# A quarter of the taps moved ahead of the filter's load in a convolution kernel with an MLP

## The chip, the cores and the metric

The kernel runs on one core of a Trainium2 chip. The time is that of the device for one launch, in microseconds; the median of three runs is given. The profile is one execution of the same program, recorded by the hardware profiler; its span (202.2 us for the kernel before) is a little shorter than the time measured for the same execution (204.36).

## The reference

Two blocks follow one another on x of 2048 tokens by 512 channels, in bfloat16. Only the first part of the first block matters here: k is filtered with four taps along the tokens, multiplied by v, and the product kv is convolved with a filter as long as the sequence, by way of the Fourier transform.

```python
for t in range(ks):                                   # ks = 4
    k_shift = k_shift + k_pad[:, t:t + S, :] * shift_k[:, ks - 1 - t][None, None, :]
kv = k_shift * v
...
y_f = kv_f * kf_f[None, :, :, :]                      # rfft of kv and of ssm_k, padded to 2 S
y = irfft(y_f)[:, 0, :S, :] + kv * ssm_D
h = x + layernorm(x) * y
out = h + relu(layernorm(h) @ w1) @ w2                # w1: 512 x 1376
```

## The kernel before

Everything is written in one function, and each engine takes its instructions in the order in which the code issues them; no scheduler moves them. The function can be read as stages.

**Loads.** One DMA brings the filter ssm_k (2 MB) into `sk`. On ScalarE's queue the tap weights `wsh` (4 KB) are loaded. Then k and v follow on the sync queue in quarters of 512 tokens, each by a transposing DMA, in the order k0, v0, k1, v1, k2, v2, k3, v3 (tiles `kT` and `vT`, lines 113 to 118), so that channels lie on partitions. `draw` (ssm_D) is last.

**Warm-up and tables.** TensorE runs 22 matmuls on zeros (`warm`). VectorE and GpSimd make integer "turns", and ScalarE makes the sine tables of the Fourier transform from them: `c2s` from `w_ts` (two pieces, 22 and 10 rows), `c2c` from `w_tc` (two pieces of 16 rows, turns by `cc_turns`), each piece by two activations. `cc_part()` issues the next activation of a list, and six of them are spread over the loop below. GpSimd makes the identity, the four diagonal tap matrices `wdiag` (identity times tap weights, line 238), the tables `f_hi` and `f_lo`, and the negated sines `c2n` (line 250).

**First transposes.** `to_rows` (line 277) is called eight times on `sk`: four TensorE transposes of 128x128 into a PSUM tile `pst`, evicted into `kfl` by VectorE or ScalarE ("DADDADAD"). The tiles come from a ring of three places of two banks each, except for two calls, which use the two tap banks.

**The loop.** For gb from 0 to 7: `taps(gb // 2, gb % 2)` multiplies half of a quarter of k by its tap matrices into the two tap banks (eight matmuls), and VectorE multiplies each bank by v and writes kv over `sk` (line 372, called the product with v below). `stage1` for gb takes two places of the ring and runs 64 small matmuls on `kfl`; its first half is evicted by ScalarE, its second by ScalarE for even gb and by VectorE for odd gb (lines 259 and 261). With three places, gb 0 holds places 0 and 1, gb 1 holds 2 and 0, gb 2 holds 1 and 2, and so on, so a turn shares one place with the turn before it.

```python
    for gb in range(8):
        taps(gb // 2, gb % 2)
        stage1(kfl, a1k_of, gb, ("AA", "AD")[gb % 2], pairs=(gb == 2))
        if gb < 6:
            cc_part()
```

**Second transposes and the rest.** `to_rows` is called eight more times, now on kv, into `xfl`. Each transpose takes words from all quarters, so all of kv must be written first. Stage 1 of kv and stage 2 of the filter, the products in frequency, the inverse transforms, the layer norms and the MLP (`ps1m`, `ps2m`) follow.

Of the kernel before, what the change touches and what calls it, by code (L numbers as in the profile page):

```python
# [9 lines left out]
ALU = mybir.AluOpType  # L10
BF16 = mybir.dt.bfloat16
F32 = mybir.dt.float32
F32R = mybir.dt.float32r
I32 = mybir.dt.int32
PSUM = bass.MemoryType.PSUM
P = 128
# [25 lines left out]
def _turns(nc, out, r, col, M, quarter):  # L42

    nc.vector.tensor_scalar(out=out, in0=r, scalar1=col, scalar2=float(M // 2 + (M // 4 if quarter else 0)),
                            op0=ALU.mult, op1=ALU.add)
    nc.vector.tensor_single_scalar(out=out, in_=out, scalar=M - 1, op=ALU.bitwise_and)
# [10 lines left out]
def kernel(  # L57
# [13 lines left out]
    nc = tc.nc  # L71
    _, S, D = A_q.shape
    DFF = B_w1.shape[1]
    KS = A_shift_k.shape[1]
    assert S == 2048 and D == 512 and KS == 4, "kernel is specialised to S=2048, D=512, ks=4"
    NT = 16
    DC = D // P
# [10 lines left out]
    early = pl.push("early")  # L88
    wp = pl.push("wp", side="right")
    kvp = pl.push("kvp", side="right")  # L90
    psum = pl.push("psF", space=PSUM)
    psum_t = pl.push("psT", space=PSUM)


    sk = early.tile([P, DC, S], BF16, name="sk")
    nc.sync.dma_start(out=sk[:], in_=A_ssm_k.rearrange("(c p) t -> p c t", p=P))
    wsh = consts.tile([P, DC, KS], BF16, name="wsh")
    nc.scalar.dma_start(out=wsh[:], in_=A_shift_k.rearrange("(r p) j -> p r j", p=P))
    dtab = consts.tile([P, 64, DC], BF16, name="dtab")
    draw = consts.tile([P, DC, 64], BF16, name="draw")  # L100
    vT = [vp.tile([P, DC, 512], BF16, name=f"vT{c}") for c in range(4)]
    CH = 512
    kT = [(kvp if c < 2 else early).tile([P, DC, CH + 16], BF16, name=f"kT{c}") for c in range(4)]
    wdiag = kvp.tile([P, DC, KS, P], BF16, name="wdiag")

    idle = vT[3][:, 0, :]
    nc.vector.memset(idle, 0.0)
    warm = psum_t.tile([P, 512], F32, tag="pk0", name="warm")
    for _ in range(22):
        nc.tensor.matmul(out=warm[:], lhsT=idle[:, 0:P], rhs=idle, start=True, stop=True)  # L110

    nc.vector.memset(kT[0][:, :, 0:16], 0.0)
    for c in range(4):
        if c == 0:
            nc.sync.dma_start_transpose(out=kT[c][:, :, 16:CH + 16], in_=k_d[0:CH, :])  # L115
        else:
            nc.sync.dma_start_transpose(out=kT[c][:], in_=k_d[CH * c - 16:CH * c + CH, :])  # L117
        nc.sync.dma_start_transpose(out=vT[c][:], in_=v_d[CH * c:CH * c + CH, :])  # L118
    for dp in range(2):
        src = bass.AP(tensor=A_ssm_D.tensor, offset=A_ssm_D.offset + 64 * dp, ap=[[0, 64], [P, DC], [1, 64]])  # L120
        nc.sync.dma_start(out=draw[64 * dp:64 * dp + 64, :, :], in_=src)
# [17 lines left out]
    def _sin(out, turns, M, neg=False):  # L139

        nc.scalar.activation(out=out, in_=turns, func=ACT.Sin, scale=(-TURN if neg else TURN) / M,
                             bias=(pbias if neg else nbias)[:])
# [4 lines left out]
    r1 = early.tile([P, 32], I32, name="f1_r")  # L147
    nc.gpsimd.iota(r1[:], pattern=[[2, 32]], base=1, channel_multiplier=0)
    n2i = early.tile([P, 1], I32, name="n2i")
    for s in range(0, P, 64):  # L150
# [4 lines left out]
    ident = consts.tile([P, P], BF16, name="ident")  # L155
    nc.gpsimd.memset(ident[:], 0.0)
    nc.gpsimd.affine_select(out=ident[:], in_=ident[:], compare_op=ALU.not_equal, fill=1.0,
                            base=0, pattern=[[-1, P]], channel_multiplier=1)
    ident32 = early.tile([P, P], F32, name="ident32")
    nc.gpsimd.tensor_copy(out=ident32[:], in_=ident[:])  # L160

    n1c = early.tile([P, 1], F32, name="n1c")
    n2c = early.tile([P, 1], F32, name="n2c")
# [14 lines left out]
    def at_k1(tab, k1):  # L178
        a, t = [p for p in tab if p[0] <= k1][-1]
        return t[:, k1 - a, :]  # L180

    tsn = early.tile([P, 32, 64], I32, name="w_ts")
    tcs = early.tile([P, 32, 64], I32, name="w_tc")
    ta = early.tile([P, 96], F32, name="w_ta")
# [3 lines left out]
    def wrap(t, M):  # L188
        nc.vector.tensor_single_scalar(out=t, in_=t, scalar=M - 1, op=ALU.bitwise_and)
# [13 lines left out]
    for dp in range(2):  # L203
        table(cs[0], tsn, dp)

    t1 = early.tile([P, 64], I32, name="f1_t")
    _turns(nc, t1[:, 0:32], r1[:], n1c[:], 128, True)
    _turns(nc, t1[:, 32:64], r1[:], n1c[:], 128, False)
    f1f = early.tile([P, 64], F32, name="f1_f")
    f1p = f1f[:].rearrange("p (k s) -> p s k", s=2)  # L210
    _sin(f1p[:, 0], t1[:, 0:32], 128)
    _sin(f1p[:, 1], t1[:, 32:64], 128, neg=True)
    t3 = early.tile([P, 2, 64], I32, name="dm_t")
    _turns(nc, t3[:, 0, :], r2[:, 32:96], n2s[:], 64, True)
    _turns(nc, t3[:, 1, :], r2[:, 32:96], n2s[:], 64, False)
    dsc = early.tile([P, 2, 64], F32, name="dm_f")
    cs_turns(*cs[1])
    cc_parts = [(cs[1], tsn, dp) for dp in range(2)] + [(p, tcs, dp) for p in cc for dp in range(2)]

    def cc_turns(a):  # L220
        part = tcs[:, a:a + 16, :]
        nc.vector.tensor_single_scalar(out=part, in_=tsn[:, a:a + 16, :], scalar=2048.0, op=ALU.add)
        wrap(part, 8192)

    def cc_part():
        table(*cc_parts.pop(0))

    cc_turns(0)

    f1hi = early.tile([P, 64], BF16, name="f1_hi")  # L230
    f1lo = early.tile([P, 64], BF16, name="f1_lo")
# [2 lines left out]
    for f in (f2hi, f2lo):  # L234
        nc.gpsimd.memset(f[:], 0.0)

    for rg in range(DC):
        nc.gpsimd.tensor_tensor(out=wdiag[:, rg, :, :], in0=ident[:].unsqueeze(1).to_broadcast([P, KS, P]),
                                in1=wsh[:, rg, :].unsqueeze(2).to_broadcast([P, KS, P]), op=ALU.mult)
        if rg == 1:  # L240
            nc.gpsimd.tensor_copy(out=f1hi[:, 0:64], in_=f1f[:])
            nc.gpsimd.tensor_tensor(out=f1f[:], in0=f1f[:], in1=f1hi[:, 0:64], op=ALU.subtract)
            nc.gpsimd.tensor_copy(out=f1lo[:, 0:64], in_=f1f[:])
    for f, g in ((f1hi, f2hi), (f1lo, f2lo)):
        for rg in range(DC):
            rows = slice(32 * rg, 32 * rg + 32)
# [1 line left out]
    def negated(a, b):  # L248
        (ao, to), (ai, ti) = [[p for p in tab if p[0] <= a][-1] for tab in (cn, cs)]
        nc.gpsimd.tensor_single_scalar(out=to[:, a - ao:b - ao, :], in_=ti[:, a - ai:b - ai, :].bitcast(F32), scalar=-1.0,  # L250
                                       op=ALU.mult)
# [19 lines left out]
    def bank2(name):  # L271
        return place([P, 2, 512], F32, name)
# [4 lines left out]
    def to_rows(word, q, fl, eng):  # L277
        shape = [P, 4, P]
        pst = tap_bank(q % 5 - 3, shape, F32, "pst") if word is sk_word and q % 5 > 2 else place(shape, F32, "pst")
        for i in range(4):  # L280
            nc.tensor.transpose(out=pst[:, i, :], in_=word(4 * q + i), identity=ident32[:])  # L281
        if eng == "D":
            fl32 = fl[:].rearrange("p g d n -> p (g d n)").bitcast(I32).rearrange("p (g d m) -> p g d m", g=64, d=2)
            nc.vector.tensor_single_scalar(out=fl32[:, :, :, 4 * q:4 * q + 4],
                                           in_=pst[:].bitcast(I32).rearrange("p m (d g) -> p g d m", d=2),
                                           scalar=0, op=ALU.bitwise_or)
        else:
            src = pst[:].rearrange("p m x -> p (m x)").bitcast(BF16).rearrange("p (m d g e) -> p d g m e", m=4, d=2, e=2)
            for d in range(2):
                nc.scalar.copy(out=fl[:, :, d, 8 * q:8 * q + 8].rearrange("p g (m e) -> p g m e", e=2), in_=src[:, d])  # L290
# [43 lines left out]
    kfl = early.tile([P, 64, 2, 64], BF16, name="kfl")  # L334
# [4 lines left out]
        return sk32[:, :, m]  # L339

    for q in range(8):
        to_rows(sk_word, q, kfl, "DADDADAD"[q])
    cc_turns(16)
    _sin(dsc[:], t3[:], 64)
    dre = consts.tile([P, 2, 2, 64], F32R, name="dre")
    dim = consts.tile([P, 2, 2, 64], F32R, name="dim")
    nc.gpsimd.memset(dre[:].bitcast(F32), 0.0)
# [14 lines left out]


    kvp2 = sk[:].rearrange("p c t -> p (c t)").rearrange("p (m c a e) -> p m c a e", m=32, c=DC, e=2)
    def taps(c, h):
        pss = [tap_bank(i, [P, 512], F32, "pkv") for i in range(2)]
        for i in range(2):
            for j in range(KS):
                nc.tensor.matmul(out=pss[i][:], lhsT=wdiag[:, 2 * h + i, j, :],  # L369
                                 rhs=kT[c][:, 2 * h + i, 16 - j:CH + 16 - j], start=(j == 0), stop=(j == KS - 1))  # L370
        for i in range(2):
            nc.vector.tensor_tensor(out=kvp2[:, :, 2 * h + i, 8 * c:8 * c + 8, :].rearrange("p m a e -> p a m e"),
                                    in0=pss[i][:].rearrange("p (a m e) -> p a m e", a=8, e=2),
                                    in1=vT[c][:, 2 * h + i, :].rearrange("p (a m e) -> p a m e", a=8, e=2),
                                    op=ALU.mult)

    for gb in range(8):
        taps(gb // 2, gb % 2)
        stage1(kfl, a1k_of, gb, ("AA", "AD")[gb % 2], pairs=(gb == 2))
        if gb < 6:  # L380
            cc_part()
        if gb == 1:
            negated(22, 32)
    pl.pop("psT")
    places.append(pl.push("psX", space=PSUM))
    ring[:] = [1, 3, 2, 0]
# [23 lines left out]
    for k4 in range(8):  # L410
        ks = slice(4 * k4, 4 * k4 + 4)
        for s in range(2):
            ps = bank2("ps2k")
# [428 lines left out]
```

## Time and profile before

| | |
|---|---|
| time, median of 3 | 204.28 us (204.13 to 207.29) |
| span of the profiled execution | 202.2 us |
| TensorE busy | 192.2 us, 95% |
| VectorE, ScalarE, GpSimd busy | 144.8, 128.6, 85.5 us |
| granted TensorE clock, mean | 0.995 |
| from the start to the second transposes | 34.9 us: TensorE busy 31.2, VectorE 27.7, ScalarE 25.5, GpSimd 27.1 |
| from there to the end | 167.3 us: TensorE busy 161.0 |

The last two rows are sums over stretches of time. A busy share says how much of a stretch an engine had an instruction in it, and not that it was the bound: in the first stretch four engines and the DMAs are all busy most of the time, and what ends it has to be read from the chain of waits and from the rows of each engine. PE is TensorE, DVE VectorE, ACT ScalarE, POOL GpSimd, SPq the sync engine as it issues DMAs; L with a number is a line of the kernel.

### The profile page before, as it was taken

The page shows a single profiled execution, that of the slowest core. Times are in us where ns is not written, and L with a number is a line of the kernel's source. Part 1 is how long each engine was busy: PE and PEld are TensorE (multiplying, and loading weights), DVE is VectorE, ACT ScalarE, POOL GpSimd, SP SyncE. Part 2 cuts the span into 40 slices and gives each one's busy share as a digit, 9 for nine tenths or more (in the row PEclk, how much of TensorE's full clock was granted, in tenths as well). Part 3 has the DMA queues.
Part 4 walks back from the last instruction along what each step waited for, and adds up shares of the span by engine and source line. Part 5 has one row for each costly group of instructions (what it writes and reads, how often), then busy time and mean ns, then how long its engine had stood idle before and what let it go on. Part 6 is the DMA issues. An engine that isn't in the chain of part 4 may idle for free.

```text
span 202.2 us, 5318 instructions
## 1 busy us (share of the span) xinstructions
PE 192.2 (95%) x2209; PEld 136.3 (67%) x2209; DVE 144.8 (72%) x238; ACT 128.6 (64%) x199; POOL 85.5 (42%) x121
## 2 busy tenths in 40 slices
PE   7897999999988999999999999999999999999991
PEld 2474545999977998988998877545664556544451
DVE  7988677888887998898994798958477117652131
ACT  2668898778785888885979964925570583026300
POOL 7199995000016999994959284200120002002000
PEclk9999999999999999999999999999999999999998
DMA  5999991000000007809981889754381602140011
GB/s 178 335 216 167 177 174 37 3 5 3 6 3 2 0 16 194 275 25 215 273 189 22 108 87 190 140 104 108 83 156 51 109 0 52 33 92 34 0 52 52
DMA packets 48491, 20.05 MB, mean 99 GB/s; under 512 B 43380, under 2 KB 46932, under 8 KB 48468
## 3 DMA queue, kind: packets, MB, share of 16 engines
q1 hardware_dynamic: 47940, 19.71, 47.5%
q8 instruction: 17, 0.28, 0.6%
q10 hardware_dynamic: 528, 0.00, 0.1%
q14 instruction: 6, 0.05, 0.1%
HBM read 7.08 MB, written 2.10 MB: 45 GB/s over the span
## 4 chain that ended last, share of the span: by engine, by line
PE 78%; SPq 11%; DMA 3%; DVE 3%; ACT 2%; issue 1%; ACTq 0%
PE ps1m L714 19%; PE ps2m L744 19%; PE psy L462 7%; PE psi L609 7%; PE ps2k L328 4%; SPq L118 4%; SPq L115 4%; PE ps2k L330 4%; PE u L328 4%; PE u L330 3%; SPq L117 3%; DMA kT<-in_A_k_dram 3%; PE pz L687 3%; PE ps L310 2%; PE pst L281 2%; PE pkv L369 2%
## 5 line engine op out<-in xcount | busy, mean ns | idle before, releaser
L729 ACT ACTIVATE h1T<-ps1m 128x512 bf16<-128x512 f32 (+1 forms) x44 | 25.7, 597 | 35.8 <-PE ps1m L714 35.7
L714 PE MATMUL ps1m<-xT,w 128*128 128x512 bf16 (+2 forms) x192 | 43.7, 365 | 0.4 <-DVE xT L660 0.4
L744 PE MATMUL ps2m<-w,h1T 128*128 128x512 bf16 (+3 forms) x187 | 40.8, 368 | 0.0
L687 PE MATMUL pz<-bd,ax 128*128 128x128 f32 x96 | 35.7, 410 | 0.0
L452 POOL TENSOR_TENSOR t<-usb,kf 128x320 fp32r<-128x320 f32 x32 | 28.2, 942 | 2.2 <-ACT usb L448 1.7
L452 DVE TENSOR_TENSOR t<-u,kf 128x704 fp32r<-128x704 f32 x32 | 26.7, 885 | 3.3 <-ACT usb L448 3.2
L748 DVE SCALAR_TENSOR_TENSOR o<-ps2m,rstd,xh 128x512 bf16<-128x512 f32 (+1 forms) x17 | 12.1, 717 | 22.2 <-PE ps2m L744 11.5
L744 PEld LDWEIGHTS <-h1T 128*128 128x128 bf16 (+1 forms) x187 | 16.2, 98 | 16.0
L553 POOL TENSOR_SCALAR rstd<-mv 128x4 f32<-128x4 f32 x8 | 2.5, 318 | 57.3 <-DVE mv L551 57.3
L259 ACT CAST a<-ps 128x1024 fp32r<-128x1024 f32 (+1 forms) x22 | 22.4, 1054 | 3.6 <-PE ps L310 3.6
L714 PEld LDWEIGHTS <-w 128*128 128x128 bf16 (+1 forms) x192 | 15.9, 100 | 12.1 <-DVE xT L660 0.5
L687 PEld LDWEIGHTS pz<-bd,ax 128*128 128x128 f32 x96 | 18.5, 193 | 7.6
L547 DVE BATCH_NORM_STATS2 st<-xh 128x6 f32<-128x512 bf16 x32 | 19.9, 677 | 0.6 <-DMA xh<-xT 0.6
L658 DVE TENSOR_TENSOR qT<-pz,qT 128x1024 bf16<-128x1024 f32 x8 | 9.8, 1220 | 13.6 <-PE pz L687 10.8
L259 ACT CAST kf<-psy 128x512 fp32r<-128x512 f32 x30 | 17.4, 641 | 1.8 <-PE psy L462 0.2
L537 ACT ACTIVATE bd<-ecw,nbias 32x512 fp32r<-32x512 int32 x24 | 17.3, 719 | 0.6
L369 PE MATMUL pkv<-kT,wdiag 128*128 128x512 bf16 x64 | 15.2, 380 | 1.5 <-POOL f_hi L247 1.0
L462 PE MATMUL psy<-t,ipos 128*128 128x512 f32 x48 | 16.0, 393 | 0.0
L261 DVE CAST a<-ps 128x1024 fp32r<-128x1024 f32 (+1 forms) x12 | 13.6, 1137 | 2.6 <-PE ps L310 2.5
L259 ACT CAST ax<-psi 128x1024 fp32r<-128x1024 f32 x13 | 12.4, 1015 | 3.7 <-PE psi L609 3.7
L609 PE MATMUL psi<-dre,kf 128*128 128x256 f32 x60 | 14.6, 286 | 0.0
L609 PE MATMUL psi<-dim,kf 128*128 128x256 f32 x60 | 14.3, 280 | 0.0
(132 smaller groups left out, 393.5 us busy)
## 6 DMA issues: line engine op xcount, KB each, us to landing
sk<-in_A_ssm_k_dram SPq DMA_DIRECT2D x1, 2048.0 KB
xh<-in_A_q_dram SPq DMA_DIRECT2D x16, 128.0 KB
out_dram<-o SPq DMA_DIRECT2D x15, 128.0 KB
w<-in_B_w_dram SPq DMA_DIRECT2D x1, 1376.0 KB
w<-in_B_w_dram SPq DMA_DIRECT2D x1, 1280.0 KB
xh<-xT SPq DMA_TRANSPOSE x8
out_dram<-o SPq DMA_DIRECT2D x2, 64.0 KB
w<-in_B_w_dram SPq DMA_DIRECT2D x1, 96.0 KB
```

Of the source, the lines that this page charges most:

```text
L259: nc.scalar.copy(out=o, in_=i)
L328: nc.tensor.matmul(out=ps[:, kk, :], lhsT=at_k1(w_re, k1), rhs=a_in(2 * k1), start=True, stop=False, skip_group_check=True)
L369: nc.tensor.matmul(out=pss[i][:], lhsT=wdiag[:, 2 * h + i, j, :], rhs=kT[c][:, 2 * h + i, 16 - j:CH + 16 - j], start=(j == 0), stop=(j == ...
L452: eng.tensor_tensor(out=t[:, :, j, :], in0=in0.unsqueeze(1).to_broadcast([P, 2, n, 2]), in1=kfr[:, :, j, ks], op=ALU.mult)
L462: nc.tensor.matmul(out=psy[:], lhsT=m_[:], rhs=t_.rearrange("p j k -> p (j k)"), start=first, stop=not first)
L537: nc.scalar.activation(out=bd[h][rows, :, :, rg, :], in_=ecw[q % 2][rows, :, 256 * h:256 * h + 256].rearrange("p b (j n) -> p b j n", n=32 ...
L547: nc.vector.bn_stats(out=st[:, i, :], in_=src[:, i, :])
L609: nc.tensor.matmul(out=banks[i // 2][:, i % 2, :], lhsT=kf[:, c, 4 * m:4 * m + 4, :].rearrange("p r k -> p (r k)"), rhs=d[:].rearrange("p ...
L687: nc.tensor.matmul(out=pz[:, il, :, a, :], lhsT=ax[:, 64 * rho + n2, :, :].rearrange("p d g -> p (d g)"), rhs=bd[h][:, rho, 4 * il + a, :, ...
L714: nc.tensor.matmul(out=ps1[fc][:fsz, 128 * ii.start:128 * ii.stop].rearrange("p (i t) -> p i t", t=P), lhsT=w1[:, c, fc * P:fc * P + fsz], ...
L729: nc.scalar.activation(out=h1T[:fsz, fc, :], in_=ps1[fc][:fsz, :], func=ACT.Relu)
L744: nc.tensor.matmul(out=ps2[:, 0:w], lhsT=h1T[:ksz, fc, i * P:(i + 1) * P], rhs=w2[:ksz, fc, ds], start=(fc == 0), stop=(fc == NFC - 1))
```

## The change

The tap weights move to the head of the sync queue, and k0 is loaded ahead of ssm_k. The taps of quarter 0, all four channel groups, run before the first transposes; VectorE copies their result from PSUM to a tile `ks0` in SBUF. v0 is loaded last, and only the four products of `ks0` with v0 remain for it, at the end of the loop, two on VectorE and two on GpSimd. Quarters 1 to 3 use turns 0 to 5 of the loop, and turns 6 and 7 have no taps. wdiag is made earlier on GpSimd, ahead of the fp32 identity. Three of the six sines in the loop, and both pairs of turns for them, move ahead of the first transposes; one of the evictions of `kfl` goes from ScalarE to VectorE. The warm-up becomes 10 matmuls before the taps and 8 after them. The purpose is that the work behind the last load is small, and that TensorE and ScalarE use the time in which ssm_k is still on its way.

```diff
-    nc.sync.dma_start(out=sk[:], in_=A_ssm_k.rearrange("(c p) t -> p c t", p=P))
-    nc.scalar.dma_start(out=wsh[:], in_=A_shift_k.rearrange("(r p) j -> p r j", p=P))
+    nc.sync.dma_start(out=wsh[:], in_=A_shift_k.rearrange("(r p) j -> p r j", p=P))
...
+    warm_up(10)
...
+    load_k(0)
+    nc.sync.dma_start(out=sk[:], in_=A_ssm_k.rearrange("(c p) t -> p c t", p=P))
+    for c in (1, 2, 3):
+        load_k(c)
+        load_v(c)
+    load_v(0)
...
+    for rg in range(DC):
+        nc.gpsimd.tensor_tensor(out=wdiag[:, rg, :, :], in0=ident[:].unsqueeze(1).to_broadcast([P, KS, P]),
+                                in1=wsh[:, rg, :].unsqueeze(2).to_broadcast([P, KS, P]), op=ALU.mult)
     ident32 = early.tile([P, P], F32, name="ident32")
...
+    tap0 = [psum_t.tile([P, 512], F32, tag=f"pk{i}", name="tap0") for i in range(2)]
+    tap0b = psum.tile([P, 2, 512], F32, tag="ps2", name="tap0b")
+    for rg in range(DC):
+        tap_products(tap0[rg], 0, rg)
+    warm_up(8)
...
+    for rg in range(2):
+        nc.vector.tensor_copy(out=ks0[:, rg, :], in_=tap0[rg])
+    cc_part()
+    cc_part()
     cc_turns(0)
+    for rg in range(2, 4):
+        nc.vector.tensor_copy(out=ks0[:, rg, :], in_=tap0[rg])
+    cc_part()
+    cc_turns(16)
...
-        to_rows(sk_word, q, kfl, "DADDADAD"[q])
-    cc_turns(16)
+        to_rows(sk_word, q, kfl, "DADDADDD"[q])
...
+    negated(22, 32)
     for gb in range(8):
-        taps(gb // 2, gb % 2)
+        if gb < 6:
+            taps(1 + gb // 2, gb % 2)
         stage1(kfl, a1k_of, gb, ("AA", "AD")[gb % 2], pairs=(gb == 2))
-        if gb < 6:
+        if gb < 3:
             cc_part()
-        if gb == 1:
-            negated(22, 32)
+    for rg in range(DC):
+        by_v((nc.vector, nc.gpsimd)[rg % 2], 0, rg, ks0[:, rg, :])
```

The small table of the 128-point transform (`f_t`, `f_f`) is also made ahead of the large ones on VectorE and ScalarE, and the turns tile `dm_t` is overwritten in place by its sine.

## The prediction

> **What bounds the kernel now.** I read the page's engine table first: TensorE is busy 95% of the span, so I looked for the stage in which it isn't the bound. The slices show one: in the first six (30 us) the DMAs are at 5 to 9 tenths, and then nearly idle for the next seven. Then the chain of waits, first 39 us:
>
> ```profile
> 1.26 7.64 SPq L115
> 8.94 2.10 SPq L118
> ...
> 23.17 6.27 DMA kT<-in_A_k_dram
> 29.48 1.92 PE pkv L369 x8
> 31.42 0.70 DVE sk L372
> 32.16 1.91 PE pkv L369 x8
> 34.09 0.70 DVE sk L372
> 34.79 0.14 issue
> 34.93 3.88 PE pst L281 x32
> ```
>
> Columns are start, length, what. The transposing loads carry the chain until the last quarter of k lands at 29.44; two groups of taps and stage 1 follow, and at 34.93 the second transposes (those of kv) begin. From there TensorE hardly stops and the diff touches nothing. So the change is worth what it does to the start of these transposes; call it T, now 34.93.
>
> The timeline of the loop, PE rows first:
>
> ```profile
> 26.92 1.89 PE L369 MATMUL pkv<-kT,wdiag 128*128 128x512 bf16 x8 [0.25 <-DVE sk L372]
> 28.74 0.21 PE L310 MATMUL ps<-f_hi,kfl 32*128 32x64 bf16 x4
> ```
>
> Taps to stage 1 is 1.82 us; the next taps start at 29.48, so stage 1 takes 0.74. The bracket says that these taps waited for a tap bank, which VectorE frees by multiplying with v. The VectorE and ScalarE rows:
>
> ```profile
> 13.02 0.69 DVE L284 TENSOR_SCALAR kfl<-pst 128x512 int32<-128x512 int32 x1 [0.21 <-PE pst L281]
> 13.62 1.33 DVE L222 TENSOR_SCALAR w_tc<-w_ts 128x1024 int32<-128x1024 int32 x1
> ...
> 26.17 1.29 DVE L372 TENSOR_TENSOR sk<-pkv,vT 128x512 bf16<-128x512 f32 x2 [0.59 <-DMA vT<-in_A_v_dram]
> ...
> 34.77 1.23 DVE L261 CAST a<-ps 128x1024 fp32r<-128x1024 f32 x1
> ```
>
> ```profile
> 30.85 1.32 ACT L193 ACTIVATE c2c<-w_tc,hbi,hsc 128x1024 fp32r<-128x1024 int32 x1
> 32.06 2.06 ACT L259 CAST a<-ps 128x1024 fp32r<-128x1024 f32 x2
> 34.73 1.14 ACT L259 CAST a<-ps 128x1024 fp32r<-128x1024 f32 x1 [0.60 <-PE ps L310]
> ```
>
> kfl is complete at 13.7; v's third quarter lands at 26.17 and its product releases the taps of 26.92 (0.75 later); a ScalarE eviction of one stage 1 half takes 1.03 (2.06 for two), VectorE's 1.23, a 128x1024 sine 1.15 from start to next start. Last, the waits:
>
> ```profile
> POOL wdiag L238 <- DMA wsh<-in_A_shift_k_dram: 4.5, 1, 4.5
> ```
>
> GpSimd had to wait for the tap weights, 4 KB, until 9.3, about when the 2 MB of ssm_k landed (9.15).
>
> **What the Trainium skill says.** "DMA: Bandwidth & Descriptors", section "Queues, rings and completion order": each DMA engine takes turns between the queues that have work, and takes one queue's descriptors in order. The trace agrees: on ScalarE's own queue wsh finished with ssm_k; at the head of the sync queue it should come first. "VectorE: DVE Perf Modes", "The perf-mode tier table": tensor_tensor with bf16 in SBUF runs at 2x, with a PSUM operand at 1x. The trace has only the PSUM form (0.69), so this bounds the new SBUF products. "GPSIMD Engine Reference", "1. Specifications": GpSimd shares SBUF interfaces with VectorE. The trace fits: the same 128x1024 tensor_scalar took 0.69 at 8.22 and 1.33 at 13.62, while GpSimd built wdiag.
>
> **The change, part by part.**
>
> *Loads.* Same bytes. wsh's issue costs about 0.5 us (ssm_k's took 0.47). kT0's issue, no longer behind 2 MB, should take 2.1 to 2.7 (the free rows of 8.94 and 11.09). ssm_k is issued 2.7 to 3.2 after its old 0.72 and, at its old 8.4 us to landing, is there at 11.9 to 12.3; with the DMAs already running it may be 11. I take 11.8, was 9.15. Six transposing loads took 26.17 - 9.15 = 17.0 after ssm_k; now the sixth after it is v's last quarter: 11.8 + 17.0, and 0.1 for the additional rows of k: **v3 lands at 28.9**, v0 2.85 later at 31.75.
>
> *Taps of quarter 0.* 16 matmuls (two groups of 1.82, 3.6 us) leave the loop for the start. wsh should land at about 3.5 (between 2, as the last output store's wait of 1.9 suggests, and 9.3); four wdiag products of 1.09 end at 7.9, the taps at 8.9. Eight warm-up matmuls follow; four fewer in all. Hidden: ssm_k isn't there yet. Even wsh 2 us later would end before 11.8.
>
> *VectorE ahead of kfl.* It gains four copies ks0 (4 x 0.69 from PSUM) and the second cosine pair (L222 and L189, 1.4), formerly after kfl. From the trace's start-to-start times: 2.25, f_t 0.71, ta 0.43, the 22-row turns 2.74, dm_t 0.79, the 10-row turns 1.26, which is 8.2, or up to 8.8 with GpSimd beside it; two copies 9.7; pair 11.1; two copies 12.5; pair 13.9. Only then come its evictions of kfl, six now, not five, at 0.68: **kfl complete at 18.0**, was 13.7. So VectorE, not ssm_k, sets it (TensorE could transpose from 11.8).
>
> *ScalarE.* Three sines leave the loop: -3.45 us there. They hide ahead of ssm_k. One kfl eviction leaves too.
>
> *The loop.* Stage 1 of gb 0 ends at 18.75. ScalarE then has six evictions and three sines until the first half of gb 3 is out: 18.75 + 6 x 1.0 + 3 x 1.15 = 28.2. gb 4's stage 1 needs that place (ring of three, two a turn: gb 3 holds 0 and 1, gb 4 wants 2 and 0) and ends at 28.95. gb 5's taps need a tap bank that is freed by the product with v3: 28.9 + 0.75 = 29.65. The loads decide, narrowly.
>
> *The tail.* gb 6 and gb 7 have no taps between them now, so each waits for places: gb 6 takes 0 and 1, of which 1 holds gb 5's first half; gb 7 takes 2 and 0, of which 0 holds gb 6's first half. From gb 5's taps: 1.82; stage 1 0.74; ScalarE 1.03; 0.06 to react; stage 1 0.74; ScalarE 1.03; 0.06; stage 1 0.74; VectorE's cast of gb 7's second half 1.23. Sum 7.45. Behind that cast, in VectorE's order, wait its two products with v0. They have been ready since 31.75. At 0.35 (2x) to 0.69 each I take 1.0 for both, then 0.15 to react. **T = 29.65 + 7.45 + 1.0 + 0.15 = 38.25**, 3.3 us later. GpSimd's two products (1.04 to 1.23 for its bf16 512-element form) end near 34 and wait for nobody; its later dre, ones and dtab work (4.8 us in the trace, 29.08 to 33.88) ends by 39, ahead of the first use of dtab (5.1 us after T in the trace).
>
> Moving taps ahead removes 3.6 us of TensorE work from the loop, but what the loop then needs are places and VectorE's order. Forecast: 204.28 + 3.3 = **207.6 us**, 1.6% slower.
>
> **Rivals.**
> 1. *The loads set the end (faster).* If the places do not hold TensorE up, T is v0's landing plus two GpSimd products: 31.75 + 2.2 + 0.15 = 34.1, 0.8 us earlier: **203.4**. For it: only multiplications follow the last load. Against it: the cast that stands ahead of two of them, and gb 7's place.
> 2. *In between.* If kfl is complete at 17 and v3 at 27.5, TensorE leaves gb 4 at about 27.9 and T is near 36.5: **205.9**. It needs ssm_k at 10.4, so it asks for nearly no cost of the load put ahead of it.
> 3. *Slower by over 2%.* If kT0 and ssm_k hold each other up, ssm_k at 13 puts v3 at 30.1 and T at 39.5: **208.8**. If GpSimd slows VectorE's cosine work too, kfl goes to 19.5 and gb 4 to 30.4: T is then 39.0. For it: the loads' later issues took 2.9 to 3.7 us, and the DMAs moved only 8 GB/s from 18 to 19 us and 14 from 22 to 23. Against: the total of bytes is the same.
>
> **How the numbers follow.** Forecast 0.50, rival 1 0.13, rival 2 0.18, rival 3 0.19. The costs I could not read, wsh's landing (3.5, hidden), the SBUF product (0.7 to 1.4 for two) and ssm_k's landing (11 to 12.6) move T by -0.5 to +0.8 around 38.25, that is 207.1 to 208.4. For 8 in 10 I reach down through rival 2 to 204.8 and up through most of rival 3 to 209.0; rival 1 and the far end of rival 3 are left out. Slower by over 2% means above 208.4: rival 3, 0.19. Faster by over 2% would need 200.2, a T below 31, before v0 has landed: 0.03, for a mechanism that I do not see. The rest, 0.78, is within 2%.
>
> **What would show it.** Right: the last kfl row of VectorE ends near 18, not 13.7; v3's product near 28.9; TensorE idle by about 1 us each ahead of the stage 1 of gb 6 and gb 7, released by ScalarE's cast; two short VectorE products directly ahead of the second transposes, which begin near 38; everything after it shifted equally. Wrong: second transposes before 36, GpSimd's product or the landing of v0 as their releaser, kfl done before 16, or a difference that arises after them.

## The result and the profile after

The changed kernel took 227.33 us (median of four executions; 226.18 to 229.35) beside 204.56 for four of the kernel before: a ratio of 1.113, with a 95% interval of 1.105 to 1.121. The span of the profiled execution grew from 202.2 to 225.4 us, and the mean granted clock of TensorE fell from 0.995 to 0.939. The prediction, 207.6 with a range up to 209.0, missed by nearly 20 us.

The chain of waits of the kernel after, columns as before (start, length, what):

```profile
4.04 7.83 SPq L119
...
21.33 4.88 DMA vT<-in_A_v_dram
26.26 3.60 PE warm L110 x8
29.96 4.67 PE pst L312 x32
...
53.76 1.23 DVE a L292
54.98 0.94 DVE sk L396 x2
56.06 5.19 PE pst L312 x32
```

Up to 29.96 this is a new chain: the loads down to v's last quarter, then the eight matmuls on zeros, then the *first* transposes. In the kernel before, these began at 9.15:

```profile
9.15 3.83 PE L281 MATMUL pst<-ident,sk 128*128 128x128 f32 x32 [0.81 <-DMA sk<-in_A_ssm_k_dram]
```

The second transposes begin at 56.06 and not at 34.93, so 21.1 us of the 23.2 that the span grew are there by then.

The first rows of the waits in the first 62 us (who waited for whom: us in total, times, longest):

```profile
PEld L110 <- DMA vT<-in_A_v_dram: 17.2, 1, 17.2
ACT kfl L321 <- PE pst L312: 17.2, 2, 16.9
PE warm L110 <- DMA vT<-in_A_v_dram: 16.7, 1, 16.7
DVE kfl L315 <- PE pst L312: 14.9, 2, 14.2
```

One wait, 17 us long, of the warm-up (L110) for a load of v; ScalarE and VectorE, which evict the transposes, stand idle behind it. TensorE's timeline says the same:

```profile
8.49 1.04 PE L178 MATMUL tap0b<-kT,wdiag 128*128 128x512 bf16 x4 [0.23 <-POOL wdiag L171]
26.26 3.60 PE L110 MATMUL warm<-vT 128*128 128x512 bf16 x8 [16.73 <-DMA vT<-in_A_v_dram]
29.96 4.67 PE L312 MATMUL pst<-ident,sk 128*128 128x128 f32 x32
```

Why a warm-up on zeros waits for v is in the code: its operand is a part of the tile that v's last quarter is loaded into.

```python
    idle = vT[3][:, 0, :]
    nc.vector.memset(idle, 0.0)
```

The program orders each instruction after the last one written ahead of it that writes what it reads. Before, all 22 warm-up matmuls stood in the code ahead of the loads, and it was the load that had to wait for them, at no cost: they ended at 8.34, and it was issued at 26.19. After, the second eight stand *behind* the load of `vT[3]`; they read what that load writes, and so must wait for it. Nothing uses their result.

The page's slices, 5.6 us each, show the hole, and what it did to the clock:

```profile
PE   7600399973999979999999998999999999999992
PEclk9955569996799999999999999999999999999999
```

The granted clock falls in the hole, and again in the tenth and eleventh slices, ahead of and in the second transposes.

### The profile page after: what moved, and what is told of

Its sections match the earlier page's. It is cut to its first block, busy times and chain, and to the rows that moved or that the text cites. A ratio compares the mean times of both kernels' runs of the same rounds, so it can differ in the third digit from the quotient of the medians.

```text
span 225.4 us, 5298 instructions
## 1 busy us (share of the span) xinstructions
PE 195.0 (87%) x2194; PEld 138.7 (62%) x2205; DVE 148.9 (66%) x241; ACT 128.2 (57%) x197; POOL 89.7 (40%) x123
## 4 chain that ended last, share of the span: by engine, by line
PE 80%; SPq 9%; ACT 4%; DVE 3%; DMA 2%; issue 1%; ACTq 0%
PE ps1m L746 17%; PE ps2m L776 17%; PE psy L494 7%; PE psi L641 6%; SPq L119 5%; PE pkv L178 5%; PE ps L341 5%; PE pst L312 4%; PE ps2k L359 4%; PE ps2k L361 3%; PE u L359 3%; PE u L361 3%; PE pz L719 3%; DMA vT<-in_A_v_dram 2%; SPq L122 2%; PE warm L110 2%
## 5 line engine op out<-in xcount | busy, mean ns | idle before, releaser
L776 PE MATMUL ps2m<-w,h1T 128*128 128x512 bf16 (+3 forms) x181 | 40.2, 368 | 0.2
L746 PEld LDWEIGHTS <-w 128*128 128x128 bf16 (+1 forms) x192 | 15.9, 100 | 12.5 <-DVE xT L692 0.9
L110 PE MATMUL warm<-vT 128*128 128x512 bf16 x18 | 7.6, 600 | 17.9 <-DMA vT<-in_A_v_dram 16.7
L110 PEld LDWEIGHTS <-vT 128*128 128x128 bf16 x18 | 2.3, 139 | 22.2 <-DMA vT<-in_A_v_dram 17.2
```

The lines of the kernel that those rows point to most:

```text
L746: nc.tensor.matmul(out=ps1[fc][:fsz, 128 * ii.start:128 * ii.stop].rearrange("p (i t) -> p i t", t=P), lhsT=w1[:, c, fc * P:fc * P + fsz], ...
L776: nc.tensor.matmul(out=ps2[:, 0:w], lhsT=h1T[:ksz, fc, i * P:(i + 1) * P], rhs=w2[:ksz, fc, ds], start=(fc == 0), stop=(fc == NFC - 1))
```

## The experiments

Each ratio is to the kernel before as it ran on the same chip as the experiment, and intervals are 95%. Each profile is of one execution.

**1. The load behind the warm-up.** The kernel after, with the issue of v's last two loads (and of ssm_D) moved in the code behind `warm_up(8)`. Every engine and queue keeps its instructions and their order; only the direction of that one dependence is turned.

```diff
-    for c in (1, 2, 3):
+    for c in (1, 2):
         load_k(c)
         load_v(c)
-    load_v(0)
+    load_k(3)
...
     warm_up(8)
+    load_v(3)
+    load_v(0)
```

> The change with one edit: the load of v's last quarter (and those behind it) stands after the second warm-up in the code, so that the warm-up's matmuls on zeros read vT3 before the load writes it; every engine and the DMA queue keep the same instructions in the same order. Theory W (the wait of these matmuls for v3's load is the loss): first transposes begin near 11.5, VectorE completes kfl near 21, the second transposes begin near 41, total 209 to 212 us. Theory O (the new order of loads and taps is itself slow): total stays above 220 us. Theory C (TensorE's lower clock is the loss, whatever made it idle): above 215 us.

Measured: 212.22 us, ratio 1.035 (1.030 to 1.039). TensorE's timeline of this kernel:

```profile
9.37 1.89 PE L110 MATMUL warm<-vT 128*128 128x512 bf16 x8
12.24 1.13 PE L314 MATMUL pst<-ident,sk 128*128 128x128 f32 x8 [0.98 <-DMA sk<-in_A_ssm_k_dram]
15.04 4.59 PE L314 MATMUL pst<-ident,sk 128*128 128x128 f32 x24 [1.67 <-DVE ks L263]
...
40.87 6.20 PE L314 MATMUL pst<-ident,sk 128*128 128x128 f32 x32 [2.41 <-DVE sk L398]
```

The warm-up runs at 9.37, while ssm_k is on its way, as it was meant to; the first transposes begin at 12.24 and the second at 40.87, 15.2 us earlier than in the kernel after. So the wait is worth 15 us, two thirds of the loss. What is left, 7.6 us against the 204.63 of the kernel before on this chip, is not the wait. The rows show where it lies: the second transposes start 5.9 us later than before (40.87 against 34.93) and take 2.3 us longer (6.20 against 3.88). The other experiments look into these two.

**2. No second warm-up.** `warm_up(8)` is left out of the kernel after.

> The change without its second warm-up of 8 matmuls, all else as in the change. Theory W: the same gain as when the load is moved behind it, total 209 to 212 us, with TensorE idle from about 9.5 to 11.5 and at most 1 us lost to a lower clock. Theory C: an idle TensorE goes to half clock and the first transposes take 5 us or more instead of 3.9, total above 215 us. Theory O: above 220 us.

Measured: 212.74 us, ratio 1.040 (1.037 to 1.043), its second transposes at 40.91. Taking the waiting instructions away gives what turning the dependence gave. Only the first eight transposes differ:

```profile
12.36 1.94 PE L311 MATMUL pst<-ident,sk 128*128 128x128 f32 x8 [2.82 <-DMA sk<-in_A_ssm_k_dram]
```

They took 1.94 us, and 1.13 behind a warm-up that ran: the second warm-up does do something for the clock, but as TensorE has a later wait for `ks` there, it is not seen in the time.

**3. One such matmul in the kernel before.** The converse: the wait alone, without the rest of the change. Here the order of the loads is the old one, with v's last quarter last.

```diff
+    nc.tensor.matmul(out=warm[:], lhsT=idle[:, 0:P], rhs=idle, start=True, stop=True)
     TURN = 2.0 * math.pi * SIN_SHRINK
```

> The kernel before with one more warm-up matmul on vT3, written behind the loads in the code, so that it waits for v's last quarter ahead of the first transposes. Theory W: first transposes begin near 31.5 instead of 9.15, second transposes near 56, total 225 to 228 us, all of the loss with none of the change's reordering. Theories O and C: no more than 5 us slower than before (C: unless the idle time drops the clock, then up to 210 us).

Measured: 225.26 us in a single run, so without an interval, its span 223.1. A single matmul of 0.61 us made the span of the kernel before 20.9 us longer:

```profile
29.52 0.61 PE L124 MATMUL warm<-vT 128*128 128x512 bf16 x1 [21.32 <-DMA vT<-in_A_v_dram]
29.92 5.10 PE L282 MATMUL pst<-ident,sk 128*128 128x128 f32 x32
```

What counts is not what the instruction costs, but what is queued behind it on its engine.

**4. Filling TensorE's pauses.** The theory for the longer transposes (6.20 us) was the granted clock. Experiment 1, by windows of 1 us (window, share of the core's time, then PE, PEld, DVE, ACT and POOL busy with their counts, granted clock, DMA share, GB/s):

```profile
38.00:39.00 1.00, 0.47 (x61) 0.36 (x45) 0.43 (x1) 1.00 (x2) 0.00 (x0) 1.00 0.00 0
39.00:40.00 1.00, 0.00 (x0) 0.00 (x0) 1.00 (x2) 0.70 (x1) 0.00 (x0) 0.61 0.00 0
...
41.00:42.00 1.00, 1.00 (x6) 1.00 (x7) 0.00 (x0) 0.00 (x0) 0.00 (x0) 0.50 0.00 0
...
46.00:47.00 1.00, 1.00 (x11) 1.00 (x10) 0.69 (x1) 0.81 (x2) 0.00 (x0) 0.98 0.00 0
```

At clock 0.50 six transposes fall into a microsecond, at 0.98 ten (the eleventh matmul there is of the next stage). From the mean of its window, the clock is halved at about 39.2, after TensorE's pauses in the tail of the loop, and it stays so until about 46.0. The Trainium skill, "TensorE: Matmul & The Clock Gate", section "What's actually happening", says that the clock is halved after an idle window of about 3.4 us and released after about as much sustained work. The trace agrees in kind; here 5.2 us of transposes (40.87 to 46.0) ran before the release, and 3.1 in the kernel after (56.06 to 59.2), and the clock fell after pauses with work between them: TensorE was busy for 0.01, 0.67, 0.19, 0.47 and 0.00 of the microseconds from 35 to 40. To test it, matmuls whose result nothing reads fill the pauses of experiment 1:

```diff
+    def fill(n):
+        junk = tap_bank(0, [P, 512], F32, "junk")
+        for _ in range(n):
+            nc.tensor.matmul(out=junk[:], lhsT=wdiag[:, 0, 0, :], rhs=kT[3][:, 0, 16:CH + 16], start=True, stop=True)
...
     for gb in range(8):
+        if gb >= 6:
+            fill(4)
...
+    fill(8)
```

> As the run with the load behind the warm-up, with TensorE kept busy at the loop's end by matmuls whose result nobody reads: 4 each ahead of the stage 1 of gb 6 and gb 7 and 8 ahead of the second transposes, all where TensorE waits anyway. Theory K (TensorE's thin use from 35 to 40 us halves its clock, and the second transposes pay for it): clock 1.0 throughout, second transposes 3.9 us instead of 6.2, total 209.5 to 211 us, 1.5 to 2.5 below the 212.2 of the run without them. Rival: the transposes are slow for another reason, or the added matmuls delay stage 1: 212 us or more.

Measured: 210.37 us, ratio 1.026 (1.021 to 1.030), 1.85 us less than experiment 1. The page's clock row, and the second transposes:

```profile
PEclk9999999999999999999999999999999999999999
```

```profile
40.42 3.88 PE L314 MATMUL pst<-ident,sk 128*128 128x128 f32 x32
```

Exactly the 3.88 us of the kernel before. So about 2 us of the remaining 7.6 are the clock. The two profiles differ ahead of the loop too, where their code is the same: in experiment 1 the clock was also halved during the first transposes (15.3 to 18.7; 24 of them took 4.59 us), and in this execution it was not. TensorE came to the loop 0.5 us earlier for it, so up to that much of the 1.85 may not be owed to the filling.

**5. A fourth place for the tail.** In experiment 1, the tail from the taps of gb 5 (32.30) to the second transposes is a chain of waits for places and for VectorE:

```profile
34.84 1.11 ACT a L292
...
35.99 0.74 PE ps L343 x62
36.73 1.03 ACT a L292
...
37.81 0.74 PE ps L343 x62
...
38.57 1.23 DVE a L294
39.80 0.94 DVE sk L398 x2
```

Stage 1 of gb 6 and of gb 7 (L343) each stand behind a ScalarE eviction, and VectorE's cast and its two products with v0 come last. Here the products with v0 are issued ahead of the taps of gb 5, and gb 6 and gb 7 get a fourth place from the tap banks, which are free by then.

```diff
     for gb in range(8):
+        if gb == 5:
+            for rg in range(DC):
+                by_v((nc.vector, nc.gpsimd)[rg % 2], 0, rg, ks0[:, rg, :])
+        if gb == 6:
+            pl.pop("psT")
+            places.append(pl.push("psX", space=PSUM))
+            ring[:] = [0, 3, 1, 2]
```

> As the run with the load behind the warm-up, and the end of the loop loosened: the products with v0 are issued ahead of gb 5's taps, and the two tap banks become a fourth place of the ring from gb 6 on, so that stage 1 of gb 6 and gb 7 need not wait for the eviction before. Theory P (places and VectorE's order hold the tail up, and the idle TensorE then runs the second transposes at half clock): second transposes begin near 37 instead of 40.9 and take 3.9 us instead of 6.2, total 206 to 208 us. Theory L (the late kfl is all of what is left): within 1 us of 212.

Measured: 208.26 us, ratio 1.013 (1.010 to 1.016): 4.0 us less than experiment 1. The transposes:

```profile
37.35 5.33 PE L314 MATMUL pst<-ident,sk 128*128 128x128 f32 x32
```

They begin 3.5 us earlier, and the clock costs a little less, though 5.33 us is not the 3.9 that was expected. (The profiled execution took 212.27 us, 4.0 over the median. Its extra time lies later: from the end of these transposes it took 167.8 us, and experiment 1 took 163.8.) The tail was the greater part of what the wait left; which of the two edits gave more was not tried apart.

**6. The diagonal tap matrices on VectorE.** VectorE's rows in the kernel after, which experiment 1 has too:

```profile
3.07 1.02 DVE L219 TENSOR_SCALAR w_ta<-w_r,n2c 128x32 f32<-128x32 int32 x1
4.01 1.09 DVE L220 TENSOR_SCALAR w_ta<-w_r,n2c 128x64 f32<-128x64 int32 x1
5.14 2.40 DVE L232 TENSOR_TENSOR w_ts<-w_ta 128x1408 int32<-128x1408 f32 x1
7.57 1.61 DVE L223 TENSOR_SCALAR w_ts<-w_ts 128x1408 int32<-128x1408 int32 x1
```

From `w_ta` to the end of `w_ts` is 6.0 us, while GpSimd builds `wdiag` (3.00 to 8.44); in the kernel before, which built it later, it was 3.2. To see whether GpSimd is the cause, experiment 1 with `wdiag` on VectorE. The block stands ahead of `w_ta` in the code now, and the taps, the warm-up and the last loads follow it:

```diff
     for rg in range(DC):
-        nc.gpsimd.tensor_tensor(out=wdiag[:, rg, :, :], in0=ident[:].unsqueeze(1).to_broadcast([P, KS, P]),
+        nc.vector.tensor_tensor(out=wdiag[:, rg, :, :], in0=ident[:].unsqueeze(1).to_broadcast([P, KS, P]),
```

> As the run with the load behind the warm-up, and the four wdiag products made by VectorE ahead of its large turns, not by GpSimd beside them. Theory G (GpSimd's wdiag slowed VectorE, 6.0 us for ta and the 22-row turns against 3.2 in the kernel before): these take 3.2 us again, the products about 0.5 each, VectorE reaches kfl about 1 us earlier, and the total falls by 0.5 to 1.5 us. Rival: VectorE is slow there for another reason, the four products only add to its queue, and the total rises by about 2 us.

Measured: 212.73 us, ratio 1.035 (1.028 to 1.043): no gain.

```profile
3.07 2.78 DVE L208 TENSOR_TENSOR wdiag<-ident,wsh 128x512 bf16<-128x512 bf16 x4
...
6.19 1.62 DVE L234 TENSOR_TENSOR w_ts<-w_ta 128x1408 int32<-128x1408 f32 x1
7.85 0.90 DVE L225 TENSOR_SCALAR w_ts<-w_ts 128x1408 int32<-128x1408 int32 x1
```

The same turns ran in 2.9 us (5.77 to 8.66), so GpSimd's four products did cost VectorE 3 us. This agrees with what the prediction took from the Trainium skill ("GPSIMD Engine Reference", "1. Specifications"), that GpSimd shares SBUF interfaces with VectorE, and it is larger than the prediction allowed. But building `wdiag` itself takes VectorE 2.8 us (0.69 each), and two later `w_tc` rows grew from 0.70 to 1.41: it reached `kfl` at 17.24, and at 16.78 in experiment 1. That GpSimd's products slow VectorE is shown, and this is no cure.

**7. The second cosine pair behind `kfl`.** Experiment 1 with `cc_turns(16)` back where the kernel before had it, and its eviction order "DADDADAD".

> As the run with the load behind the warm-up, and VectorE relieved ahead of the first transposes: the second pair of cosine turns goes back behind the evictions of kfl, and one of these goes back to ScalarE. Theory V (once the wait is gone, VectorE's queue ahead of kfl sets the loop): kfl complete 2 to 2.6 us earlier and the total 2 us lower than with the load moved alone. Theory L (loads or the places of the ring set the end of the loop): within 0.7 us of it.

Measured: 211.94 us, ratio 1.039 (1.032 to 1.045): a miss. I had expected `kfl` earlier by the pair; it came at 20.34, and at 20.56 in experiment 1. TensorE's rows:

```profile
15.04 4.58 PE L313 MATMUL pst<-ident,sk 128*128 128x128 f32 x24 [1.82 <-DVE ks L263]
...
23.86 1.89 PE L175 MATMUL pkv<-kT,wdiag 128*128 128x512 bf16 x7 [1.91 <-DVE sk L398]
```

The third transposed tile needs the place in which half of the early taps lies until VectorE has copied it to `ks0`, at 15.0 in both kernels. And in the profiled execution the pair, now ahead of VectorE's first products with v, holds the taps of gb 1 up by 1.9 us; this execution took 214.08 us, 2.1 over the median, so whether the others have that wait too is not shown.

**8. All together.** Experiments 1, 5 and 6, with the copies to `ks0` on ScalarE ahead of its sines, evictions "DDADDADD", and the second cosine pair and five sines in the loop.

> All three together, with the four ks0 copies on ScalarE ahead of its sines, the second cosine pair on VectorE back in the loop, and five sines in the loop instead of three. If the wait, VectorE's queue ahead of kfl and the tail are the whole loss: kfl complete near 17, second transposes near 34, total 203 to 205 us, level with the kernel before or a little faster. If the order of the loads costs something of its own: above 207 us.

Measured: 207.14 us, ratio 1.009 (1.006 to 1.011). TensorE ran all first transposes at once and `kfl` was complete at 16.7, where 17 was expected; but the second transposes began at 36.41, where 34 was expected. The first row is TensorE's; the second, of VectorE, shows where the rest went:

```profile
11.99 3.83 PE L309 MATMUL pst<-ident,sk 128*128 128x128 f32 x32 [1.09 <-DMA sk<-in_A_ssm_k_dram]
```

```profile
31.36 1.96 DVE L393 TENSOR_TENSOR sk<-ks,vT 128x512 bf16<-128x512 bf16 x2 [1.24 <-DMA vT<-in_A_v_dram]
```

With the loop this early, v0 isn't there yet, and VectorE waits for it with the products of gb 5 queued behind. Above 207 us was to mean that the order of the loads costs something of its own; this wait for the load that was moved to the end is such a cost. The two products are also slow, 1.96 us: GpSimd's two ran beside them (31.39 to 34.21).

**9. The products a little later.** Experiment 8 with those products behind stage 1 of gb 5.

> As the combined run, with the products with v0 issued behind gb 5's stage 1 instead of ahead of gb 5's taps, so that VectorE no longer waits for v0 with gb 5's products queued behind. If that wait (1.2 us, and 2 us of products beside GpSimd's) set the combined run's end: second transposes begin near 34.5 instead of 36.4, total 1 to 2 us below it, level with the kernel before. If the ring's places set it: no change.

Measured: 205.90 us beside 204.81 before, ratio 1.004 (1.002 to 1.006). The second transposes begin at 35.23, in pieces:

```profile
35.23 0.63 PE L309 MATMUL pst<-ident,sk 128*128 128x128 f32 x4 [0.53 <-issue]
36.13 0.66 PE L309 MATMUL pst<-ident,sk 128*128 128x128 f32 x4 [0.27 <-ACT a L287]
37.11 2.84 PE L309 MATMUL pst<-ident,sk 128*128 128x128 f32 x24 [0.32 <-ACT a L287]
```

They end at 39.95, and in the kernel before at 38.81. This is the best form of the change that was found, and still 0.4% slower than the kernel before.

**10. Experiment 9 with six filling matmuls ahead of gb 6.**

> The same with 6 matmuls on a tap bank ahead of gb 6's stage 1, whose result nobody reads. Theory K: the clock stays at 1.0 and the second transposes take 3.9 us, about 1 us less in total than the run without them, 203 to 205 us. Rival: the matmuls delay gb 6 by as much as the clock gives: no difference.

Measured: 206.33 us, ratio 1.006 (1.004 to 1.009). No gain. There may have been little to give: in the profiled execution of experiment 9 (205.39 us) the clock is at 1.00 throughout the second transposes, though the mean clock of its other executions goes down to 0.987. Whether the filling delays gb 6, as the rival has it, was not looked into.

## Why the prediction was wrong

**The step that failed** is in the part on the taps of quarter 0: "Eight warm-up matmuls follow; four fewer in all. Hidden: ssm_k isn't there yet." I counted the matmuls, and did not ask what they read: a wait of 17 us stood in the sum at nothing. It is in no rival either, so the whole set of cases, and the range with it, lay far below the result. Experiments 1, 2 and 3 show the step wrong from three sides: turned round, the wait gives back 15 us; without the matmuls the same; and one such matmul alone costs the kernel before 20.9 us of its span.

**Without the wait** the forecast would still have been low, 207.6 against the 212.22 of experiment 1. Two of its terms were mis-sized there:

- *VectorE ahead of kfl.* 13.9 was forecast, 16.78 measured. The turns with `w_ta` were taken at 0.43 + 2.74 = 3.17 us and took 6.04 beside GpSimd, which is the whole 2.9. The prediction had read "or up to 8.8 with GpSimd beside it", which allowed 0.6, and named slower cosine work in rival 3. `kfl` was thus complete at 20.56 and not at 18.0. "TensorE could transpose from 11.8" also holds only for the first eight transposes: the rest need the place of half of the early taps, which VectorE's second copies to `ks0` give back, at 15.00 where the working has 12.5. From 15.04 on TensorE works without a wait for 17.26 us, up to the taps of gb 5 at 32.30, which were forecast for 29.65. So "The loads decide, narrowly" is wrong. The chain of experiment 1 at that point:

```profile
13.79 1.21 DVE ks L263 x2
...
15.04 4.59 PE pst L314 x24
```

- *The clock.* The prediction took the second transposes to last as long as before. They took 2.3 us more, as the tail with its pauses, which it did describe, let the clock fall (experiment 4).

Together: 38.25 + 2.6 = 40.85 for the start of the second transposes (40.87 measured), and 204.6 + 5.9 + 2.3 = 212.8 for the time. That the first sum comes out so well is in part luck. The forecast reached 29.65 by way of v's last quarter; TensorE's 17.26 us from 12.5 on would have led, by estimate, to 29.8, so two different paths happened to give nearly the same time.

**What held.** The tail: 7.45 + 1.0 + 0.15 = 8.6 us from the taps of gb 5 to the second transposes; 8.57 in experiment 1, and 8.87 in the kernel after (47.19 to 56.06). Its two products took 1.02 us. In the kernel after, the products with v0 were not held by the load, and rival 1 falls. The landing of `wsh` was hidden. v's last quarter landed at 26.26, not at 28.9, which moved nothing in the forecast's favour, since TensorE waited for exactly that. Two of the signs named for "right" failed: `kfl` was done not near 18 but at 35.65, and the second transposes began at 56. The signs named for "wrong" were all for a kernel faster than forecast or for a difference behind the second transposes, and told nothing of this.

The 22.8 us of the result are thus some 15 for the wait, some 2 for the clock in the second transposes, 3.5 to 4 for the tail (experiment 5), and 2 to 2.5 for VectorE's late start on `kfl`. This last is what remains, and not measured alone: experiments 6 and 7, which aimed at it, gained nothing. The step from experiment 5 to experiment 9, 2.4 us by the medians and 1.8 by the ratios, fits it, but has the products with v0 in another place as well. The last two overlap with one another and with the clock, so the split is an estimate, good to about 1 us; experiment 9, which treats them together, comes to within 1.1 us of the kernel before.

## What to carry to other kernels

Where an instruction is moved past another in program order, ask of every tile that it reads or writes who else touches it: a dummy instruction on borrowed memory is harmless ahead of the load that fills it, and a wait for that load behind it. A cheap instruction at the head of an in-order engine costs what is queued behind it. Before work is moved to an idle stretch of one engine, look at what the other engines run beside it there, and before a loop is thinned out, at whether its pauses leave the clock up.

## What the runs showed of the hardware

- VectorE's small turns grew out of proportion beside GpSimd's bf16 products: a 128x64 tensor_scalar took 1.09 us, and 0.24 when GpSimd had no such work (experiment 6).
- VectorE's product of two bf16 SBUF tiles took 0.5 us with plain operands (two in 1.02) and 0.69 with broadcast ones (`wdiag` in experiment 6, four in 2.78). The same two plain products took 2.50 in experiment 5 and 1.96 in experiment 8, with GpSimd's two beside them (31.27 to 33.79; 31.39 to 34.21), and 1.07 in experiment 9, where GpSimd's had ended at 32.52 before they began at 33.22.
- In the kernel after, by the mean clock of the windows, the clock fell about 2 us after TensorE's last matmul (9.5), and came back 5.6 us after its work began again (26.26), in the middle of the first transposes. The return after the tail took 3.1 us of work there, and 5.2 in experiment 1, so this time is no constant:

```profile
11.00:12.00 1.00, 0.00 (x0) 0.00 (x0) 1.00 (x3) 1.00 (x1) 0.88 (x4) 0.69 1.17 89
...
31.00:32.00 1.00, 1.00 (x8) 1.00 (x7) 0.69 (x1) 0.06 (x1) 0.01 (x1) 0.57 0.00 0
32.00:33.00 1.00, 1.00 (x11) 1.00 (x10) 0.58 (x1) 1.00 (x2) 1.00 (x1) 1.00 0.00 0
```
